# Global queries of two head pairs on 128 partitions, and two passes over the weights moved to ScalarE

## The chip, the cores and the metric

One NeuronCore of a Trainium2 chip runs the whole program. The metric is the device time of one execution in microseconds; the engines are TensorE (PE), VectorE (DVE), ScalarE (ACT), GpSimd (POOL) and SyncE (SP), which issues all DMAs here.

## What is computed

The reference takes 8 batches of 8 heads with 512 local and 32 global tokens of 64 values each, and a feed-forward part on the result.

```python
s_g = scale * q_g @ k_all.T ; out_g = sm(s_g) @ v_all
s_l = concat(scale * q_l @ k_g.T, where(abs(i - j) <= 32, scale * q_l @ k_l.T, -1e9))
out_l = sm(s_l) @ concat(v_g, v_l)
x = concat(out_g, out_l) as (8, 544, 512)
u = x + real(fft over tokens and over the 512 columns of x)
un = (u - mean(u)) / sqrt(var(u) + 1e-6)
out = u + max(un @ w_ch1, 0) @ w_ch2
```

The weights w_ch1 (512 x 2048) and w_ch2 (2048 x 512) arrive as 64-bit floats; the program reads each as two 32-bit words.

## The kernel before

The kernel works with sums of two float16 parts (a high and a low one), so a product of two matrices is three matmuls. A list of tasks is made in `run`, each with an engine, an assumed duration, the tasks it needs and the buffers it takes. `Plan.order` then writes out one fixed order for each engine's queue from these and from tables of numbers (STEP, STAG, LEAD, DLEAD, BIAS, CAPS). On the chip every queue runs in that order and waits on semaphores.

Weights: 32 tiles of 128 x 512. `w_load` brings one in as pairs of 32-bit words. `w_abs` (line 356, ScalarE) writes the absolute value of the high words to PSUM. `w_bits` takes their maximum into a column (line 363, VectorE, with an accumulator) and shifts the bits left by 3 (line 364). `w_join` puts in sign and top exponent bit (line 370) and the top 3 bits of the low word (line 371). `w_max`, `w_fold`, `w_top`, `w_spread` and `w_scale` make one scale from the maxima of four tiles (w_ch1) or of all sixteen (w_ch2); `w_hi` and `w_lo` write the two float16 parts (lines 430, 432, 439).

Attention goes by pairs of heads p (32 pairs, 4 to a batch). Local queries: `scores`, `masked` (line 607, VectorE), `exps`, `p_hi`, `p_lo`, a DMA transpose `turn`, `values` (lines 642 and 644), `norm`. Values are prepared by `v_mul`, `v_hi` (line 539, ScalarE) and `v_lo` into one of two buffers vN; keys by `prep_hi` and `prep_lo` into one of two buffers kT from the third batch on. Global queries of a pair take 64 partitions (2 heads of 32): `g_scores` (lines 668 and 669 for the first two batches, 673 and 674 after), `g_max` (679 to 681, VectorE), `g_exp` (686 and 687, ScalarE), `g_hi` (690, ScalarE), `g_lo` (693, GpSimd), the DMA transpose `g_turn`, `g_values` (708) and `g_norm` (716 to 718, VectorE).

After a batch's four pairs the transforms follow (`d_odd` to `d_addv`), with the GpSimd sums ahead and `d_lo` (line 855) and `d_tail_lo` (line 882) on VectorE. Then come the layer norm (`l_stats` to `l_turn`) and the FFN: 17 chunks of 256 rows, each in 8 steps of `f_first` (line 1038), `f_hi`, `f_lo` and `f_second` (line 1056). `f_first` uses the same two PSUM buffers (`ps1`) as the weights. The attention of later batches is woven in between the FFN steps on every queue.

Of the kernel before, what the change touches and what calls it, by code (L numbers as in the profile page):

```python
# [19 lines left out]
P = 128  # L20
# [1323 lines left out]
```

## Time and profile before

| what | us |
|---|---|
| median of 3 runs (lowest, highest) | 1085.59 (1083.68, 1087.31) |
| the profiled execution's own time | 1085.01 |
| its span, first to last instruction | 1083.2 |

The rows below come from the profiled execution. Its times run from the start of its span; a time that is measured and one of the span differ by 1.8 us.

### The profile page before, as it was taken

What the parts mean: (1) busy time and instruction counts of PE and PEld (TensorE: products, weight loads), DVE (VectorE), ACT (ScalarE), POOL (GpSimd) and SP (SyncE); (2) the same over time, 40 slices, a digit from 0 to 9 for tenths busy, and PEclk for the clock granted to TensorE, in tenths of its full rate; (3) what the DMA queues carried; (4) which work ended last, traced back from release to release, by engine and by line L of the source; (5) the groups of instructions that cost most, each with busy time, mean ns of one, the idle gap of its engine ahead of it and who ended that gap; (6) DMA issues with size and microseconds to landing.
All of it is one profiled execution on the core that took longest, in us unless ns stands there. A gap on an engine that the chain in (4) does not pass through costs nothing.

```text
span 1083.2 us, 24999 instructions
## 1 busy us (share of the span) xinstructions
PE 978.0 (90%) x9683; PEld 688.2 (64%) x9683; DVE 615.5 (57%) x1766; ACT 584.8 (54%) x1250; POOL 610.9 (56%) x840
## 2 busy tenths in 40 slices
PE   3756277998999999999999979998999999999996
PEld 2535155775767766776777747675776766676664
DVE  5999998426864585477548666647435242231111
ACT  5867467985886867786778648645212111111110
POOL 5559958886968876967877785766036020010000
PEclk9865555999999999999999989998999999999999
DMA  8999867726766858594785947384412112111000
GB/s 297 257 254 252 248 162 178 156 74 142 131 154 139 201 108 187 130 208 111 160 191 96 204 93 151 62 170 81 108 50 59 21 42 59 20 40 40 1 21 20
DMA packets 249568, 137.60 MB, mean 127 GB/s; under 512 B 200577, under 2 KB 223201, under 8 KB 249449
## 3 DMA queue, kind: packets, MB, share of 16 engines
q1 hardware_dynamic: 249448, 136.01, 55.4%
q8 instruction: 76, 1.25, 0.5%
q14 instruction: 44, 0.35, 0.1%
HBM read 65.10 MB, written 18.35 MB: 77 GB/s over the span
## 4 chain that ended last, share of the span: by engine, by line
PE 77%; DVE 14%; POOL 4%; issue 2%; DMA 2%; SPq 1%; ACT 1%; POOLq 0%; DVEq 0%; ACTq 0%
PE ps L1038 31%; PE acc L1056 30%; PE S L597 3%; PE bk L642 2%; DVE pe L607 2%; PE bk L644 2%; PE psd L930 2%; DVE ht L882 1%; DVE ps L364 1%; PE S L673 1%; DVE ps L363 1%; PE pvg L708 1%; PE S L594 1%; DVE wm L371 1%; DVE ps L370 1%
## 5 line engine op out<-in xcount | busy, mean ns | idle before, releaser
L1038 PE MATMUL ps<-uh,wh 128*128 128x256 f16 x3264 | 386.0, 275 | 0.0
L1056 PE MATMUL acc<-wh,h 128*128 128x512 f16 x1632 | 377.8, 381 | 0.0
L1038 PEld LDWEIGHTS <-wh 128*128 128x128 f16 x3264 | 316.0, 99 | 52.5 <-issue 1.2
L1056 PEld LDWEIGHTS <-h 128*128 128x128 f16 x1632 | 153.9, 98 | 166.5 <-issue 3.3
L1043 ACT ACTIVATE h<-ps 128x512 f16<-128x512 f32 x136 | 80.9, 595 | 273.2 <-PE ps L1038 272.7
L1047 DVE SCALAR_TENSOR_TENSOR h<-ps,h 128x512 f16<-128x512 f32 x136 | 93.6, 688 | 219.7 <-ACT h L1043 219.6
L624 POOL TENSOR_TENSOR ph<-pe,ph 128x448 f16<-128x448 f32 x128 | 132.1, 1046 | 88.8 <-ACT ph L620 71.2
L616 ACT ACTIVATE pe<-pe,nm 128x224 f32<-128x224 f32 x256 | 101.6, 469 | 21.5 <-DVE nm L607 21.5
L607 DVE CUSTOM_DVE_ANT_0 pe<-S,msk,z 128x224 f32<-128x224 f32 x192 | 75.3, 446 | 38.5 <-PE S L597 25.8
L642 PE MATMUL bk<-vN,pl 128*128 128x65 f16 x768 | 70.5, 203 | 20.0 <-DVE x L655 11.0
L620 ACT ACTIVATE ph<-pe 128x448 f16<-128x448 f32 x128 | 68.9, 563 | 5.9 <-DMA pl<-ph 5.3
L642 PEld LDWEIGHTS <-pl 128*128 128x128 f16 x768 | 61.8, 105 | 15.1 <-DMA pl<-ph 9.4
L644 PEld LDWEIGHTS <-pl 96*128 96x128 f16 x768 | 59.4, 104 | 14.7 <-issue 11.1
L954 POOL TENSOR_TENSOR u<-u,asm 128x257 f32<-128x257 f32 x16 | 13.1, 821 | 95.8 <-DMA u<-xs 50.1
L644 PE MATMUL bk<-vB,pl 96*128 96x65 f16 x576 | 54.4, 204 | 0.0
L693 POOL TENSOR_TENSOR pgr<-pg,pgr 64x576 f16<-64x576 f32 x32 | 41.4, 1294 | 20.7 <-issue 13.0
L543 POOL TENSOR_TENSOR vN<-vf,vN 128x640 f16<-128x640 f32 x32 | 43.5, 1361 | 14.0 <-ACT vN L539 13.7
L1061 DVE SCALAR_TENSOR_TENSOR u<-acc,ve,u 128x512 f32<-128x512 f32 x34 | 25.4, 750 | 32.3 <-PE acc L1056 32.3
L597 PEld LDWEIGHTS <-qT 64*128 64x128 f16 x1152 | 35.0, 95 | 11.7 <-issue 6.8
L439 POOL TENSOR_TENSOR wh<-wm,wh 128x512 f16<-128x512 f32 x32 | 36.9, 1158 | 4.8 <-ACT wm L432 3.5
L653 DVE TENSOR_SCALAR dn<-bk,z 128x4 f32<-128x4 f32 x64 | 13.8, 215 | 43.7 <-PE bk L644 43.7
L597 PE MATMUL S<-kT,qT 64*128 64x192 f16 x576 | 36.7, 248 | 1.8 <-DVE nm L607 1.8
(203 smaller groups left out, 1621.2 us busy)
## 6 DMA issues: line engine op xcount, KB each, us to landing
qk<-in_qk SPq DMA_DIRECT2D x32, 512.0 KB
vf<-in_v SPq DMA_DIRECT2D x32, 320.0 KB
raw<-in_moe_w_ch SPq DMA_DIRECT2D x17, 512.0 KB
xs<-x SPq DMA_DIRECT2D x32, 256.0 KB
out<-u SPq DMA_DIRECT2D x16, 512.0 KB
x<-xs SPq DMA_DIRECT2D x24, 256.0 KB
u<-xs SPq DMA_DIRECT2D x24, 256.0 KB
rw<-in_moe_w_ch SPq DMA_DIRECT2D x8, 512.0 KB
```

The source lines that it names most:

```text
L543: self.nc.gpsimd.tensor_sub(vN[:, :, 1, :, 0:64], self.st[p]["vf"], vN[:, :, 0, :, 0:64])
L597: nc.tensor.matmul(ps, qT[r, a, j], kg[r, c] if o else kT[r, k0:k0 + 192], start=m == 0, stop=m == 2)
L607: nc.vector.tensor_tensor_reduce(self.per[(4 * p + j) % 4][:, h, 0:224], S[:, h, 224 * n:224 * n + 224], self.msk[:, j], z[:, 8:9], 3e38, ...
L616: nc.scalar.activation(pe[:, h, 0:224], pe[:, h, 0:224], AF.Exp, bias=nm[:, n, h:h + 1], scale=-1.0)
L620: self.nc.scalar.activation(ph[:, 0, :, 0:224], self.per[i % 4][:, :, 0:224], AF.Copy)
L624: self.nc.gpsimd.tensor_sub(ph[:, 1, :, 0:224], self.per[i % 4][:, :, 0:224], ph[:, 0, :, 0:224])
L642: nc.tensor.matmul(pv[:, j % 2, h], pl[:, 4 * a + 2 * h], vN[:, j, c, h, :], start=m == 0, stop=False)
L644: nc.tensor.matmul(pv[:, j % 2, h], pl[0:96, 4 * a + 2 * h + 1], vb, start=False, stop=m == 2)
L1038: nc.tensor.matmul(ps[:, q], wt[:, w, c0:c0 + P], uh[:, :, 4 * a + kt, :], start=n == 0, stop=n == 11)
L1043: self.nc.scalar.activation(h[:, 0], self.fps[c, fp], AF.Relu)
L1047: self.nc.vector.scalar_tensor_tensor(h[:, 1], self.fps.pop((c, fp)), 0.0, h[:, 0], op0=ALU.max, op1=ALU.subtract)
L1056: nc.tensor.matmul(self.acc_f[c, j], h[:, a, q, j * P:(j + 1) * P], self.w[1, f][:, w, :], start=f == 0 and a == 0 and w == 0, stop=f == 1 ...
```

## The change

Three things change. First, w_abs scales the absolute value by a power of two, which puts the exponent where the shift needs it, and a new pass on ScalarE, `w_low`, makes the top 3 bits of the low word from its top byte and writes them over the low word. w_bits is a plain maximum, and w_join shifts while it joins. Second, the global queries of two pairs (a group g of four heads) share 128 partitions from g_scores to g_norm; g_out has four DMAs of 32 rows instead of two, and plg one buffer instead of two. The scale of each half is copied into one column (`zg`). Third, the tables and assumed durations that set the order are others.

```diff
-STEP = 5.93
+STEP = 6.09
-STAG = (35, 18, 18)
-LEAD = (86, 30, 32)
+STAG = (35, -6, 15)
+LEAD = (86, 32, 32)
-DLEAD = (74, 6, 32)
+DLEAD = (50, 14, 32)
...
-        self.nc.scalar.activation(m.bitcast(F32), self.raw[k, i][:, :, 1].bitcast(F32), AF.Abs)
+        self.nc.scalar.activation(m.bitcast(F32), self.raw[k, i][:, :, 1].bitcast(F32), AF.Abs, scale=2.0 ** -112)
+
+    def w_low(self, k, i):
+        raw = self.raw[k, i]
+        byte = raw.rearrange("p n t -> p (n t)").bitcast(U8).rearrange("p (n b) -> p n b", b=8)[:, :, 3]
+        self.nc.scalar.activation(raw[:, :, 0], byte, AF.Copy, bias=-15.5 / 32, scale=1.0 / 32)
 
     def w_bits(self, k, i):
...
-        g = m.bitcast(F32)
-        nc.vector.tensor_scalar(g, g, 2.0 ** -15, None, op0=ALU.max, op1=ALU.max, accum_out=self.mx[k][:, j:j + 1])
-        nc.vector.tensor_scalar(m, m, 3, 0x3FFFFFF8, op0=ALU.logical_shift_left, op1=ALU.bitwise_and)
+        nc.vector.tensor_reduce(self.mx[k][:, j:j + 1], m.bitcast(F32), axis=EX, op=ALU.max)
 
     def w_join(self, k, i):
...
-        hw, lw = raw[:, :, 1], raw[:, :, 0]
-        nc.vector.scalar_tensor_tensor(m, hw, -0x40000000, m, op0=ALU.bitwise_and, op1=ALU.bitwise_or)
-        nc.vector.scalar_tensor_tensor(w, lw, 29, m, op0=ALU.logical_shift_right, op1=ALU.bitwise_or)
+        nc.vector.scalar_tensor_tensor(m, m, 3, raw[:, :, 0], op0=ALU.logical_shift_left, op1=ALU.bitwise_or)
+        nc.vector.scalar_tensor_tensor(w, raw[:, :, 1], -0x80000000, m, op0=ALU.bitwise_and, op1=ALU.bitwise_or)
...
+            zg = self.p3.tile([P, 3], F32, name="zg", bufs=3)
+            for i in range(2):
+                flip(zg[64 * i:64 * i + 64, 0:1], t[64 * i:64 * i + 64, i])
+            self.zs[g] = zg[:, 0:1]
...
+    def g_scores(self, g, alt):
...
         for m, (a, c) in enumerate(((0, 0), (0, 1), (1, 0))):
-            nc.tensor.matmul(sg, qg[:, a], kT[:, 32 + 512 * c:544 + 512 * c], start=m == 0, stop=m == 2)
-            nc.tensor.matmul(s2, qg[:, a], s["kg"][:, c], start=m == 0, stop=m == 2)
+            for r, s in zip(rows, prs):
+                nc.tensor.matmul(sg[r], self.g[s["b"]]["T"][:, a, s["hp"], 0:64], s["kT"][:, 32 + 512 * c:544 + 512 * c], start=m == 0, stop=m == 2)
+            for r, s in zip(rows, prs):
+                nc.tensor.matmul(s2[r], self.g[s["b"]]["T"][:, a, s["hp"], 0:64], s["kg"][:, c], start=m == 0, stop=m == 2)
...
-                for h in range(2):
-                    r = slice(h * SG, h * SG + SG)
-                    nc.tensor.matmul(pv[r], pl[:n, 5 * a + c, r], vN[:n, c, w, h], start=c == 0 and m == 0, stop=c == 4 and m == 2)
+                for i in range(2):
+                    vN = self.st[2 * g + i]["v"][0]
+                    for h in range(2):
+                        r = slice(64 * i + SG * h, 64 * i + SG * h + SG)
+                        nc.tensor.matmul(pv[r], pl[:n, 5 * a + c, r], vN[:n, c, w, h], start=c == 0 and m == 0, stop=c == 4 and m == 2)
```

VectorE, at its first weight tiles, before (ps1 is PSUM, mx0 the maxima, rw and raw the loaded words, wm the joined words; L607 is the mask step):

```order
L363 TENSOR_SCALAR ps1_189,mx0_92<-ps1_189 128x512
L364 TENSOR_SCALAR ps1_189<-ps1_189 128x512
L370 SCALAR_TENSOR_TENSOR ps1_189<-rw_156,ps1_189 128x512
L371 SCALAR_TENSOR_TENSOR wm_188<-rw_156,ps1_189 128x512
L363 TENSOR_SCALAR ps1_199,mx0_92<-ps1_199 128x512
L364 TENSOR_SCALAR ps1_199<-ps1_199 128x512
L363 TENSOR_SCALAR ps1_208,mx0_92<-ps1_208 128x512
L364 TENSOR_SCALAR ps1_208<-ps1_208 128x512
L370 SCALAR_TENSOR_TENSOR ps1_199<-rw_156,ps1_199 128x512
L371 SCALAR_TENSOR_TENSOR wm_198<-rw_156,ps1_199 128x512
L607 ISA pe0_86,nm_228<-S_213,msk_63,zc_99 128x224
```

and now (L368 is w_bits, L373 and L374 are w_join, L620 the mask step):

```order
L368 TENSOR_REDUCE mx0_92<-ps1_194 128x1
L373 SCALAR_TENSOR_TENSOR ps1_194<-ps1_194,rw_156 128x512
L374 SCALAR_TENSOR_TENSOR wm_193<-rw_156,ps1_194 128x512
L368 TENSOR_REDUCE mx0_92<-ps1_202 128x1
L373 SCALAR_TENSOR_TENSOR ps1_202<-ps1_202,rw_156 128x512
L374 SCALAR_TENSOR_TENSOR wm_201<-rw_156,ps1_202 128x512
L368 TENSOR_REDUCE mx0_92<-ps1_212 128x1
L373 SCALAR_TENSOR_TENSOR ps1_212<-ps1_212,raw_159 128x512
L374 SCALAR_TENSOR_TENSOR wm_211<-raw_159,ps1_212 128x512
L620 ISA pe0_86,nm_240<-S_223,msk_63,zc_99 128x224
```

Of four instructions a tile three are left, and the reduction no longer writes ps1.

ScalarE, at the same tiles, before (L356 is w_abs, L539 is v_hi, L452 sums over the global queries and keys):

```order
L356 ACTIVATE ps1_189<-rw_156 128x512
L539 ACTIVATE vN_70<-vf1_74 128x5x2x64
L356 ACTIVATE ps1_199<-rw_156 128x512
L356 ACTIVATE ps1_208<-raw_159 128x512
L356 ACTIVATE ps1_234<-raw_161 128x512
L452 ACTIVATE junk_77,accg_80<-gn_179 128x256
```

and now (L357 is w_abs, L362 is w_low):

```order
L357 ACTIVATE ps1_194<-rw_156 128x512
L362 ACTIVATE rw_156<-rw_156 128x512
L357 ACTIVATE ps1_202<-rw_156 128x512
L362 ACTIVATE rw_156<-rw_156 128x512
L362 ACTIVATE raw_159<-raw_159 128x512
L357 ACTIVATE ps1_212<-raw_159 128x512
L362 ACTIVATE raw_161<-raw_161 128x512
L357 ACTIVATE ps1_220<-raw_161 128x512
```

Each tile has a second pass, which reads and writes the loaded words in place.

TensorE, at the first FFN matmul, before (L597 is scores, L1038 is f_first):

```order
L597 LDWEIGHTS qT_1947
L597 MATMUL S_2120<-kg0_68,qT_1947 128x32
L597 LDWEIGHTS qT_1947
L597 MATMUL S_2120<-kg0_68,qT_1947 128x32
L1038 LDWEIGHTS wh_981
L1038 MATMUL ps1_2153<-uh_2071,wh_981 128x256
```

and now (L610 is scores, L407 is the last w_spread, L1058 is f_first):

```order
L610 LDWEIGHTS qT_1945
L610 MATMUL S_2040<-kg0_68,qT_1945 128x32
L610 LDWEIGHTS qT_1945
L610 MATMUL S_2040<-kg0_68,qT_1945 128x32
L407 MATMUL vm_2009<-mxr_2031,part_64 128x1
L1058 LDWEIGHTS wh_448
L1058 MATMUL ps1_2085<-uh_1984,wh_448 128x256
```

The spread of the maximum of w_ch2 has moved ahead of the first FFN matmul; before, it stood 157 rows behind it.

## Rows read from the trace of the kernel before

**Rows 1.** Busy time by stretch: stretch, length; PE, PEld, DVE, ACT, POOL; PEclk, DMA share, GB/s.

```profile
0.00:30.00 30.00, 12.52 (x60) 9.02 (x60) 16.63 (x45) 16.06 (x34) 15.76 (x32) 1.00 0.87 297
30.00:120.00 90.00, 51.64 (x591) 40.64 (x591) 84.92 (x269) 63.61 (x136) 64.27 (x68) 0.62 1.07 253
120.00:180.30 60.30, 33.22 (x326) 27.46 (x326) 56.25 (x160) 39.70 (x87) 46.51 (x52) 0.50 0.70 170
180.30:1083.20 902.90, 880.58 (x8712) 611.05 (x8706) 457.66 (x1295) 465.44 (x996) 484.40 (x691) 0.99 0.49 106
```

**Rows 2.** Chain of waits by line, 30 to 180.3 us, then 180.3 to 1083.2 us.

```profile
by line: DVE pe L607 10.9%; DVE ps L364 9.3%; DVE ps L363 9.0%; DVE wm L371 7.8%; PE S L594 7.8%; DVE ps L370 7.5%; issue 6.8%; DVE x L655 3.1%; PE S L668 2.6%; DVE ng L679 2.4%; POOL wh L439 2.3%; POOL wm L531 1.8%; DVE bst L983 1.8%; PE p
...
by line: PE ps L1038 37.0%; PE acc L1056 36.2%; PE S L597 3.4%; PE bk L642 2.1%; PE bk L644 2.0%; PE psd L930 1.8%; PE S L673 1.8%; DVE ht L882 1.7%; PE psd L900 1.5%; PE pvg L708 1.3%; issue 1.2%; DVE eh L855 0.7%; PE psd L902 0.5%; DMA pl
```

**Rows 3.** Groups by line and shape, VectorE: busy us, mean ns; idle before, releaser.

```profile
L364 DVE TENSOR_SCALAR ps<-ps 128x512 int32<-128x512 int32 x32 | 22.4, 700 | 1.1
...
L363 DVE TENSOR_SCALAR_CACHE_REDUCE ps<-ps 128x512 f32<-128x512 f32 x32 | 22.0, 689 | 2.4 <-ACT ps L356 2.4
...
L679 DVE TENSOR_REDUCE ng<-S 64x1 f32<-64x512 f32 x22 | 14.9, 678 | 8.0 <-PE S L674 7.9
...
L718 DVE TENSOR_SCALAR xg<-pvg,dng 64x64 f32<-64x64 f32 x32 | 8.8, 276 | 1.3
...
L716 DVE TENSOR_SCALAR dng<-pvg,z 64x1 f32<-64x1 f32 x32 | 6.5, 204 | 11.4 <-PE pvg L708 11.2
L681 DVE TENSOR_SCALAR ng<-ng,z 64x1 f32<-64x1 f32 x24 | 6.4, 265 | 1.0
...
L363 DVE DVE_READ_ACCUMULATOR ps<-ps 128x1 f32 x32 | 4.4, 138 | 0.0
...
L680 DVE TENSOR_REDUCE ng<-S 64x1 f32<-64x32 f32 x22 | 3.8, 173 | 0.0
```

**Rows 4.** Groups by line and shape, ScalarE.

```profile
L690 ACT ACTIVATE pgr<-pg 64x576 f16<-64x576 f32 x32 | 21.6, 676 | 4.9 <-DMA plg<-pgr 4.5
...
L686 ACT ACTIVATE pg<-S,ng,z 64x512 f32<-64x512 f32 x20 | 15.4, 771 | 10.7 <-DVE ng L681 8.1 <-POOL pgr L693 2.5
...
L432 ACT ACTIVATE wm<-wm,wsc 128x512 f32<-128x512 f32 x16 | 11.5, 722 | 0.5
...
L356 ACT ACTIVATE ps<-raw 128x512 f32<-128x512 f32 x17 | 10.6, 621 | 14.8 <-DVE wm L371 14.8
...
L687 ACT ACTIVATE pg<-S,ng,z 64x32 f32<-64x32 f32 x20 | 7.3, 363 | 0.0
```

**Rows 5.** Groups by line and shape, GpSimd.

```profile
L693 POOL TENSOR_TENSOR pgr<-pg,pgr 64x576 f16<-64x576 f32 x32 | 41.4, 1294 | 20.7 <-issue 13.0 <-ACT pgr L690 5.7 <-POOL vf L531 0.9
```

**Rows 6.** Timeline of TensorE, 305 to 320 us: start, us.

```profile
305.32 0.40 PE L673 MATMUL S<-kT,gT 128*64 128x512 f16 x1
305.56 0.18 PE L674 MATMUL S<-kg,gT 128*64 128x32 f16 x1
305.59 0.38 PE L673 MATMUL S<-kT,gT 128*64 128x512 f16 x1
...
306.17 2.79 PE L1038 MATMUL ps<-uh,wh 128*128 128x256 f16 x24
...
319.17 0.65 PE L708 MATMUL pvg<-vN,plg 128*32 128x65 f16 x30
319.75 0.50 PE L1038 MATMUL ps<-uh,wh 128*128 128x256 f16 x3
```

**Rows 7.** Chain of waits in order of time, in three stretches: start, us.

```profile
244.85 6.18 DVE eh L855
...
634.67 8.49 DVE ht L882
...
734.78 6.82 DVE ht L882
```

**Rows 8.** Waits of ScalarE: us in total, times, longest us.

```profile
ACT vN L539 <- PE bk L644: 10.0, 8, 4.4
```

More of the change, by code (lines that the diff above doesn't have):

```diff
@@ L87, in raw_home @@
     return ("x0", "x1", "uh", "uh")[n % 4] if n < 16 else "uh" if n % 5 in (0, 2) or n > 27 else "u"
-PER = {**dict.fromkeys("scores masked exps norm".split(), 8), **dict.fromkeys("p_hi p_lo turn values".split(), 16),
+PER = {**dict.fromkeys("g_scores g_max g_exp g_hi g_lo g_turn g_values g_norm".split(), 2), **dict.fromkeys("scores masked exps norm".split(), 8), **dict.fromkeys("p_hi p_lo turn values".split(), 16),
        **dict.fromkeys("s_total scales0 scales l_stats l_guess l_un l_hi l_lo l_turn l_root f_first f_hi f_lo f_second f_end f_out".split(), 2)}
-WHOLE = ("w_load", "w_abs", "w_bits", "w_join", "w_max", "w_fold", "w_top", "w_spread", "w_scale", "w_hi", "w_lo", "load_consts", "l_load")
+WHOLE = ("w_load", "w_abs", "w_low", "w_bits", "w_join", "w_max", "w_fold", "w_top", "w_spread", "w_scale", "w_hi", "w_lo", "load_consts", "l_load")
 def stage_of(key):
@@ new lines, in g_scores, with g_max @@
+            for r, s in zip(rows, prs):
+                nc.tensor.matmul(s2[r], self.g[s["b"]]["T"][:, a, s["hp"], 0:64], s["kg"][:, c], start=m == 0, stop=m == 2)
+    def g_max(self, g):
+        nc, (sg, s2) = self.nc, self.G[g]
+        ng = self.p2.tile([P, 3], F32, name="ng")
+        nc.vector.tensor_reduce(ng[:, 0:1], sg, axis=EX, op=ALU.max)
+        nc.vector.tensor_reduce(ng[:, 1:2], s2, axis=EX, op=ALU.max)
+        nc.vector.tensor_scalar(ng[:, 2:3], ng[:, 0:1], ng[:, 1:2], self.zg[g][1], op0=ALU.max, op1=ALU.mult)
+        self.G[g] = sg, s2, ng[:, 2:3]
@@ L1088, in run @@
             add(("w_abs", n), ACT, .62, self.w_abs, k, i, after=[("w_load", n)] + slot, cls=3, new=[("ps1", "w", n)], use=[r])
-            add(("w_bits", n), DVE, 1.48, self.w_bits, k, i, after=[("w_abs", n)], use=[("ps1", "w", n)])
-            add(("w_join", n), DVE, 1.4, self.w_join, k, i, after=[("w_bits", n)], use=[r, ("ps1", "w", n)])
+            add(("w_low", n), ACT, .63, self.w_low, k, i, after=[("w_load", n)], use=[r])
+            add(("w_bits", n), DVE, .68, self.w_bits, k, i, after=[("w_abs", n)], use=[("ps1", "w", n)])
+            add(("w_join", n), DVE, 1.4, self.w_join, k, i, after=[("w_bits", n), ("w_low", n)], use=[r, ("ps1", "w", n)])
             last = n % 4 == 3 if k == 0 else n == 31
@@ L1107, in run @@
             add(("w_hi", n), ACT, 1.43 if k else .71, self.w_hi, k, i, after=pre)
[L1108 removed]
+            add(("w_lo", n), POOL, 1.16 if k else 1.87, self.w_lo, k, i, after=[("w_hi", n)])
         for b in range(B):
@@ L1185, in run @@
                 add(("norm", i), DVE, .89, self.norm, i, after=[("values", 2 * i), ("values", 2 * i + 1)], use=[bk, sc] + ([x] if half else []), new=[] if half else [x], **kw)
-            G = ("A", "g", p)
-            gs, gu = ([("load", p), ("b_load", b)], [qk, gT]) if rb else ([("lo_k", p), ("halo", p), ("b_lo", b)], [kT, kg, gT])
-            add(("g_scores", p), PE, 1.0 if rb else .7, self.g_scores, p, after=gs, seq=prev("g_scores"), use=gu, new=[G], alts=[["A"], ["acc0", "acc1"]], **kw)
@@ L1189, in run @@
-            add(("g_max", p), DVE, 1.08, self.g_max, p, after=[("g_scores", p)], use=[G] if rb else [G, sc], **kw)
-            add(("g_exp", p), ACT, 1.03, self.g_exp, p, after=[("g_max", p)], seq=prev("g_exp"), use=[G] if rb else [G, sc], new=[("pg", p)], **kw)
-            add(("g_hi", p), ACT, .67, self.g_hi, p, after=[("g_exp", p)], seq=prev("g_hi"), use=[("pg", p)], new=[("pgr", p)], **kw)
-            add(("g_lo", p), POOL, 1.3, self.g_lo, p, after=[("g_hi", p)], use=[("pg", p), ("pgr", p)], **kw)
```

145 lines of the change are left out of this document (78 added, 67 removed).

## Prediction

> **What bounds the kernel now.** I read the busy time by stage first, because the average over the whole span mixes two kernels in one. Up to 180.3 us, where the first matmul of the feed-forward part (FFN) starts, VectorE is the full engine: 84.92 of 90 us and 56.25 of 60.3 us, that is 141.2 of 150.3 us or 94% from 30 us on, while TensorE is busy 84.9 of the same 150.3 us and at a granted clock of 0.62 and 0.50 [rows 1]. After 180.3 us it is the reverse: TensorE 880.6 of 902.9 us (97.5%), VectorE 457.7 (51%), ScalarE 465.4, GpSimd 484.4 [rows 1]. The chain of waits says the same. Before 180.3 us its largest entries are VectorE's mask step and the four passes over each weight tile (lines 363, 364, 370 and 371); after it the two FFN lines alone are 73% [rows 2]. So a microsecond taken from VectorE ahead of the first FFN matmul moves that start, as far as no other engine takes over; a microsecond taken from ScalarE, VectorE or GpSimd after it buys nothing by itself, and one taken from TensorE after it counts in full.
>
> **Who could take over.** From 30 to 180.3 us ScalarE is busy 103.3 us and GpSimd 110.8 us [rows 1]. The DMA engines show a busy share of 1.07 from 30 to 120 us at 253 GB/s, 22.8 MB; from 120 to 180.3 us it is 0.70 at 170 GB/s, 10.3 MB [rows 1]. The change therefore goes from an engine at 94% towards three resources at 70 to 100%.
>
> **The weights.** Per tile VectorE ran line 363 (0.689 us, plus 0.138 us for reading out its accumulator) and line 364 (0.700 us) [rows 3]. It now runs one reduction of 512 PSUM elements, for which the same operation in g_max is the row: 0.678 us [rows 3]. Saved: 0.849 us a tile, 27.2 us for 32 tiles; all 32 reductions stand ahead of the first FFN matmul in the new order. The two passes of w_join keep their shape and each still reads one operand from PSUM, so I cost their edit at nothing. ScalarE pays one more pass a tile, w_low. No row shows a byte input or an integer output. The nearest below is line 356, which reads the same tile with the same stride: 0.621 us. The nearest above is line 432, 512 floats written to SBUF: 0.722 us [rows 4]. I take 0.62, since w_low and line 356 differ in type and destination only: 19.8 us for 32 tiles, up to 23.1. The scale put into w_abs is an argument of an instruction that runs anyway, so nothing. The shorter w_max saves one operation on one to four columns, five times; I leave it at nothing.
>
> **The global queries, before the first FFN matmul.** Half as many instructions, each on 128 partitions instead of 64 and as long in the free direction. I take the duration of a VectorE, ScalarE or GpSimd instruction as unchanged by partitions; it would have to double to lose the gain. Ahead of the first FFN matmul the order before has 9 g_max and 8 g_norm, the new one 4 and 4. VectorE: 5 x (0.678 + 0.173 + 0.265) = 5.6 us and 4 x (0.204 + 0.276), the reciprocal not counted, = 1.9 us [rows 3]. The new copies of a scale add 2 small instructions for each of 4 groups, 8 x 0.204 = 1.6 us. Net for VectorE with the weights: 27.2 + 5.6 + 1.9 - 1.6 = 33.1 us. ScalarE: 9 pairs of exponentials become 4 and 8 g_hi become 4, 5 x (0.771 + 0.363) + 4 x 0.676 = 8.4 us less [rows 4]. GpSimd: 5 x 1.294 = 6.5 us less [rows 5], a few small scale instructions more; it has 40 us to spare and stays out.
>
> **Where the first FFN matmul comes to stand.** About four tiles are handled in the first 30 us, in which VectorE has 13 us idle, so of the 33.1 us 3.4 count for nothing there. After 30 us VectorE keeps 141.2 - 29.7 = 111.5 us; ScalarE gets 103.3 + 28 x 0.62 - 8.4 = 112.3 us. At the 94% that VectorE reached, both end at 30 + 119 = 149 us. The DMA engines have 33.1 MB to move in that stretch; at the 253 GB/s of the crowded stretch that takes 131 us and ends at 161 us, at the 297 GB/s of the first 30 us it ends at 141 us. Two engines at 94% side by side, each feeding the other, and DMA near its limit will not all reach their best, so I take the middle of 149 and 161: 155 us, 25.3 us earlier. The new order also puts the last fold and spread of the weights' maximum ahead of the first FFN matmul on TensorE. That makes it wait for all 32 reductions, which the sum already counts.
>
> **After the first FFN matmul.** TensorE is the bound, so its own work counts. g_scores for one pair takes 306.17 - 305.32 = 0.85 us, six matmuls of 512 and 32 columns one behind the other (0.27 us from one 512 to the next) [rows 6]. They all use 64 columns of the array, the same ones. The new code alternates between the lower and the upper 64. g_values shows what alternating gives: 30 matmuls on two groups of 32 columns take 0.58 us, 0.019 us each, where 65 streamed columns at the 0.27 us for 544 of g_scores would take 0.032 us [rows 6]; so two groups overlap to a factor of about 1.7. I take g_scores of two pairs as 0.85 us instead of 1.70. 11 of the 12 groups with this code come after the first FFN matmul: 9.4 us less. The bound on the other side is no overlap, 0. The Trainium skill, TensorEngine Tiling (Array Packing), section Available Configurations, lists 128 x 64 as two tiles, and its Key Properties say that different tiles can load and multiply in parallel; by that rule the saving would be the same 9.4 us, and no run here shows it yet at 64 columns. g_values now alternates over four groups; it lies between 0.58 and 1.16 us for two pairs, and I take no gain (bound: 12 x 0.58 = 7 us). g_max, g_exp, g_hi, g_lo and g_norm halve on engines that are 51 to 54% busy here; the FFN matmuls hide them before and after, so nothing. Were that cover gone, the other 16 - 4 groups would be worth some 1.8 us each on ScalarE.
>
> **Sum against the profiled execution.** 1083.2 - 25.3 - 9.4 = 1048.5 us span; its own time is 1085.01, 1.8 more than its span, and the median of the runs 1085.59. Forecast 1050 us.
>
> **Rivals.**
> *DMA or the mix of engines binds, and the first stage shortens little.* For it: the share of 1.07 [rows 1]. If ScalarE and VectorE reach only 80%, the FFN starts at 30 + 112.3 / 0.8 = 170 us: 1065 us.
> *The first stage is packed better than it was.* At 100% of ScalarE's 112.3 us it starts at 142 us: 1037 us. For it: VectorE did hold 94%. Against it: DMA would have to hold 296 GB/s.
> *The two column halves do not overlap.* The order and the first stage stay: 1050 + 9.4 = 1059 us.
> *The long stalls change.* Three times after 180 us TensorE waits for one VectorE instruction that takes 6.18, 8.49 and 6.82 us [rows 7]; the three sum to 21.5 us. Others of the same lines cost nothing on the chain. GpSimd is at work without a break in each. The new order rearranges these neighbours: none left gives 1050 - 21.5 = 1029 us, twice as many 1071 us. I have no row for which, and forecast three again. The Trainium skill, GPSIMD Engine Reference, section Key points, says that GpSimd shares its SBUF interfaces with VectorE and contends with VectorE instructions that have two SBUF inputs, and these three have two; by that rule such stalls stay as likely as before, since the instructions are unchanged.
> *Slower: the pair of pairs holds its buffers.* The values (two buffers) and, later, the keys (two buffers) of both pairs are now held until g_values and g_scores of the group have run. ScalarE's v_hi of the next pair waits at the head of its queue, and behind it stand the exponentials and f_hi, for which TensorE's FFN waits. Before, v_hi waited 10.0 us for the values' matmuls in 8 waits, the longest 4.4 us [rows 8]. To end above 1088 us it must cost TensorE over 38 us, 2.4 us for each of 16 groups. Against it: ScalarE has half its time free after the start. w_low as the culprit would need 1.6 us an instruction, 2.6 times line 356.
> *The change does nothing it says* has no place here: the instructions are gone from the order.
>
> **How the numbers follow.** Forecast (1042 to 1058) 0.58; first stage shortens little 0.13; packed better 0.10; no overlap of halves 0.08; stalls change 0.07; buffers, slower 0.04. I let the range run from 1036 to 1067: it takes in all but the outer stall cases and the buffers, and some of the first rival beyond 170 us. Within 0.3%, which is about what a measurement of this kernel can tell from no change, only a piece of the first and last rivals can lie: 0.02. Faster 0.94, slower 0.04.
>
> **What would show it.** In the new profile the first FFN matmul should start at 145 to 165 us, w_low last 0.62 to 0.72 us, the reduction 0.68, and VectorE and ScalarE both be 85 to 94% busy between 30 us and that start. g_scores of a group should take 0.85 to 1.0 us. From the first FFN matmul to the end should be 893 us instead of 903. If the start is later than 170 us with ScalarE below 80%, DMA or the buffers took over; if the second stretch is not shorter, the halves do not overlap or the stalls grew.

## The result, and the profile after

| | before | after |
|---|---|---|
| median of 4 runs (lowest to highest), us | 1086.1 (1083.7 to 1087.3) | 1039.4 (1037.7 to 1040.4) |
| span of the profiled execution, us | 1083.2 | 1038.2 |
| first FFN matmul, us | 180.3 | 169.7 |
| from there to the end, us | 902.9 | 868.5 |

The ratio is 0.9571 [0.9549, 0.9594]: 46.7 us less. The time lies inside the range that was given, 10.6 us below its number. But the two parts of the sum came out the other way round: the first stage gave 10.6 us instead of 25.3, and the stretch behind it gave 34.4 instead of 9.4.

Busy time by stretch of the kernel after, in the columns of [rows 1]:

```profile
0.00:30.00 30.00, 11.35 (x65) 9.00 (x65) 16.38 (x52) 18.77 (x40) 16.09 (x32) 1.00 0.96 307
30.00:169.70 139.70, 75.65 (x899) 62.74 (x899) 113.78 (x324) 113.47 (x244) 108.09 (x119) 0.57 0.96 246
169.70:1038.20 868.50, 855.27 (x8722) 597.46 (x8721) 424.11 (x1235) 440.79 (x953) 468.08 (x698) 1.00 0.50 108
```

In the middle row VectorE and ScalarE are both busy 81% of the time (113.8 and 113.5 of 139.7 us), where VectorE alone had 94% [rows 1]. Neither is full over the whole stretch any more. In the last row TensorE is busy 98.5%, at a granted clock of 1.00.

The share of 81% is an average over pieces with different limits. Three pieces of the middle row:

```profile
50.00:70.00 20.00, 11.80 (x184) 9.92 (x185) 17.51 (x58) 19.00 (x44) 19.50 (x21) 0.67 1.08 253
70.00:90.00 20.00, 10.76 (x77) 7.83 (x75) 13.02 (x39) 12.92 (x28) 13.85 (x16) 0.57 0.87 237
150.00:169.70 19.70, 9.25 (x143) 6.63 (x139) 19.09 (x44) 15.35 (x36) 16.42 (x17) 0.50 0.75 181
```

From 50 to 70 us ScalarE is at 95% and GpSimd at 98%. From 70 to 90 us no compute engine is over 70%. In the last 19.7 us VectorE is at 97%, with the layer norm, mask steps and the maximum of w_ch2 among others. One of TensorE's two longest waits of the stretch ends there, 3.6 us before the first FFN matmul, and it is for that maximum (us in total, times, longest):

```profile
PE vm L398 <- DVE mx L392: 9.2, 1, 9.2
```

The chain of waits by line, from 30 us to the first FFN matmul and behind it:

```profile
by line: DVE pe L620 9.8%; PE S L607 9.7%; DMA raw<-in_moe_w_ch 9.4%; DVE ps L373 6.5%; issue 6.2%; DVE mx L368 5.4%; DVE wm L374 5.3%; DMA pl<-ph 4.6%; DMA u<-xs 3.8%; ACT pe L629 2.4%; ACT wh L432 2.3%; DVE unh L1026 2.1%; ACT ps L357 1.7
...
by line: PE acc L1076 35.2%; PE ps L1058 35.0%; PE S L610 3.0%; PE psd L950 2.0%; PE bk L655 2.0%; PE bk L657 1.9%; DMA pl<-ph 1.8%; issue 1.3%; PE psd L920 1.2%; DMA x<-xs 1.1%; PE S L689 0.8%; DVE eh L875 0.7%; DVE un L1017 0.6%; PE pvg L
```

Against [rows 2], the four weight passes of VectorE have shrunk from 33.6% to three with 17.2%, and transfers, which did not stand among the large entries, now hold 17.8% in three entries (weights, turns, residual). No entry reaches 10%: the stage passes from engine to engine. Behind the start, `DVE ht` (1.7% in [rows 2]) is gone from the large entries.

The groups that answer to [rows 3] to [rows 5] (VectorE, ScalarE, GpSimd):

```profile
L368 DVE TENSOR_REDUCE mx<-ps 128x1 f32<-128x512 f32 x32 | 21.8, 683 | 6.3 <-ACT ps L357 6.3
L373 DVE SCALAR_TENSOR_TENSOR ps<-ps,raw 128x512 int32<-128x512 int32 x17 | 11.7, 688 | 0.0
L696 DVE TENSOR_REDUCE ng<-S 128x1 f32<-128x512 f32 x10 | 6.9, 688 | 8.4 <-PE S L691 8.4
...
L362 ACT ACTIVATE raw<-raw 128x512 int32<-128x512 uint8 x17 | 11.2, 656 | 0.0
L703 ACT ACTIVATE pg<-S,ng,zg 128x512 f32<-128x512 f32 x10 | 7.7, 765 | 0.4 <-DVE ng L698 0.2
L707 ACT ACTIVATE pgr<-pg 128x576 f16<-128x576 f32 x16 | 10.9, 681 | 0.4
...
L710 POOL TENSOR_TENSOR pgr<-pg,pgr 128x576 f16<-128x576 f32 x16 | 20.5, 1279 | 6.4 <-ACT pgr L707 4.1 <-DMA pl<-ph 2.2
```

On 128 partitions each instruction of the global queries lasts as long as it did on 64, within 2% (0.688 against 0.678, 0.765 against 0.771, 0.681 against 0.676, 1.279 against 1.294 us). The reduction takes 0.683 us (0.678 was used), and w_low 0.656 us (0.62 was used, 0.72 the bound).

TensorE's timeline of the kernel after (start, us), one g_scores group and its next matmul, then one g_values group and its next:

```profile
246.59 0.41 PE L689 MATMUL S<-kT,gT 128*64 128x512 f16 x2
246.83 0.18 PE L691 MATMUL S<-kg,gT 128*64 128x32 f16 x2
246.86 0.39 PE L689 MATMUL S<-kT,gT 128*64 128x512 f16 x2
247.08 0.18 PE L691 MATMUL S<-kg,gT 128*64 128x32 f16 x2
247.11 0.38 PE L689 MATMUL S<-kT,gT 128*64 128x512 f16 x2
247.33 0.18 PE L691 MATMUL S<-kg,gT 128*64 128x32 f16 x2
247.44 0.20 PE L655 MATMUL bk<-vN,pl 128*128 128x65 f16 x1
...
266.06 0.66 PE L726 MATMUL pvg<-vN,plg 128*32 128x65 f16 x60
266.65 0.20 PE L655 MATMUL bk<-vN,pl 128*128 128x65 f16 x1
```

From 246.59 to 247.44 are 0.85 us for two pairs; one pair alone took as long [rows 6]. And 60 matmuls of g_values take 0.59 us, where 30 took 0.58.

**Where the 34.4 us behind the start come from.** I added up the two timelines from each start on TensorE to the next, by line, idle time apart. g_scores went from 20.0 to 9.3 us (-10.7), g_values from 13.8 to 7.2 (-6.6), idle time from 12.8 to 3.7 (-9.1), the two FFN lines from 732.9 to 726.3 (-6.6). That is 33.0 of the 34.4. Groups on TensorE behind the start (busy, mean ns, idle before and what ended it), first before, then after:

```profile
L1038 PE MATMUL ps<-uh,wh 128*128 128x256 f16 x3264 | 386.0, 275 | 0.0
L1056 PE MATMUL acc<-wh,h 128*128 128x512 f16 x1632 | 377.8, 381 | 0.0
L902 PE MATMUL psd<-c1tr,ht 96*128 96x137 f16 (+1 forms) x70 | 16.0, 229 | 9.2 <-DVE ht L882 9.2
```

```profile
L1058 PE MATMUL ps<-uh,wh 128*128 128x256 f16 x3264 | 380.6, 273 | 0.1
L1076 PE MATMUL acc<-wh,h 128*128 128x512 f16 x1632 | 375.1, 379 | 0.8 <-DVE h L1067 0.8
L922 PE MATMUL psd<-c1tr,ht 96*128 96x137 f16 (+1 forms) x70 | 15.7, 225 | 1.5 <-DVE ht L902 1.5
```

The idle time that the transform's matmuls (line 902, now 922) spent on `ht` went from 9.2 to 1.5 us. The FFN matmuls are the same 3264 and 1632, yet a little shorter on average, because the stretches of a lower clock are gone: in peek_before below, which has the order of the kernel before but no such stretches, the two lines take 727.4 us. Three stretches of 30 us of the kernel before, around the long VectorE instructions of [rows 7]:

```profile
240.00:270.00 30.00, 26.40 (x275) 18.64 (x274) 17.12 (x31) 17.72 (x38) 21.07 (x22) 0.94 0.67 138
630.00:660.00 30.00, 24.11 (x243) 17.07 (x241) 21.25 (x38) 15.14 (x32) 19.17 (x21) 0.89 0.65 136
720.00:750.00 30.00, 26.71 (x258) 18.78 (x256) 21.65 (x42) 12.70 (x24) 21.41 (x29) 0.89 0.54 120
```

TensorE was idle there for 3.3 to 5.9 us, and the granted clock over the stretch is 0.94, 0.89 and 0.89: for a part of it the lower of the two levels, 1.2 GHz. In the kernel after the same three stretches of time, in which other work stands, show 30.00 us busy at 1.00.

### The profile page after: what moved, and what is told of

Its sections match the earlier page's. It is cut to its first block, busy times and chain, and to the rows that moved or that the text cites. A ratio compares the mean times of both kernels' runs of the same rounds, so it can differ in the third digit from the quotient of the medians.

```text
span 1038.2 us, 24797 instructions
## 1 busy us (share of the span) xinstructions
PE 942.3 (91%) x9683; PEld 669.2 (64%) x9683; DVE 554.3 (53%) x1609; ACT 573.0 (55%) x1234; POOL 592.3 (57%) x848
## 4 chain that ended last, share of the span: by engine, by line
PE 71%; DVE 10%; DMA 6%; POOL 5%; ACT 3%; issue 2%; SPq 1%; POOLq 0%; DVEq 0%; ACTq 0%
PE acc L1076 29%; PE ps L1058 29%; PE S L610 3%; DMA pl<-ph 2%; DVE pe L620 2%; PE bk L655 2%; PE psd L950 2%; PE bk L657 2%; PE S L607 2%; DMA raw<-in_moe_w_ch 1%; DVE ps L373 1%; PE psd L920 1%; DMA x<-xs 1%; DMA u<-xs 1%; DVE mx L368 1%
## 5 line engine op out<-in xcount | busy, mean ns | idle before, releaser
L1058 PE MATMUL ps<-uh,wh 128*128 128x256 f16 x3264 | 380.6, 273 | 0.1
L1058 PEld LDWEIGHTS <-wh 128*128 128x128 f16 x3264 | 315.2, 98 | 51.6 <-issue 0.4
L620 DVE CUSTOM_DVE_ANT_0 pe<-S,msk,z 128x224 f32<-128x224 f32 x192 | 75.0, 446 | 25.3 <-PE S L610 20.4
L607 PE MATMUL S<-qk 64*128 64x192 f32 x128 | 30.3, 562 | 22.4 <-DVE nm L620 19.8
L610 PEld LDWEIGHTS <-qT 64*128 64x128 f16 x1152 | 34.6, 94 | 9.8 <-issue 6.3
L1022 ACT ACTIVATE unh<-un 128x512 f16<-128x512 f32 x34 | 21.2, 624 | 28.0 <-DVE un L1017 27.8
L610 PE MATMUL S<-kT,qT 64*128 64x192 f16 x576 | 36.2, 246 | 0.0
```

Of the source, the lines that this page charges most:

```text
L607: nc.tensor.matmul(ps, q[r, P * j:P * j + P], kg[r] if o else kw[r, k0:k0 + 192], start=True, stop=True)
L610: nc.tensor.matmul(ps, qT[r, a, j], kg[r, c] if o else kT[r, k0:k0 + 192], start=m == 0, stop=m == 2)
L620: nc.vector.tensor_tensor_reduce(self.per[(4 * p + j) % 4][:, h, 0:224], S[:, h, 224 * n:224 * n + 224], self.msk[:, j], z[:, 8:9], 3e38, ...
L1058: nc.tensor.matmul(ps[:, q], wt[:, w, c0:c0 + P], uh[:, :, 4 * a + kt, :], start=n == 0, stop=n == 11)
```

## The experiments

My theory after the result (A): the first stage is held by engines and queues that wait for each other, no longer by one engine; and behind the start the order took away stalls that come from GpSimd working without a break beside VectorE. Its rivals: DMA bandwidth, ScalarE or VectorE alone holds the first stage; and the new instructions, not the order, took the stalls away.

"First" is the first FFN matmul and "rest" the time from there to the end of the span, both in the profiled execution. In rows from 30 us to the first FFN matmul, the columns are those of [rows 1]. Each ratio is to runs of the kernel before made beside that version; the medians of these are the range in the first line.

| kernel | median us (ratio to before) | first | rest |
|---|---|---|---|
| before | 1084.2 to 1086.1 | 180.3 | 902.9 |
| after | 1039.4 (0.957 [0.955, 0.959]) | 169.7 | 868.5 |
| w_only: weights changed, tables of before | 1088.2 (1.002 [1.000, 1.004]) | 193.7 | 893.7 |
| g_only: pairing changed, tables of before | 1071.5 (0.987 [0.983, 0.991]) | 192.2 | 873.7 |
| old_tables: whole change, tables of before | 1068.8 (0.984 [0.981, 0.988]) | 187.8 | 880.3 |
| g_apart: after, halves one behind the other | 1044.5 (0.962 [0.959, 0.966]) | 168.0 | 871.1 |
| half_after: after, half the weight bytes | 1036.5 (0.957 [0.954, 0.961]) | 165.5 | 868.3 |
| half_before: before, half the weight bytes | 1081.6 (0.998 [0.996, 1.001]) | 179.6 | 901.3 |
| extra_after: after, every second tile loaded twice | 1098.1 (1.014 [1.010, 1.017]) | 223.2 | 874.7 |
| peek_before: before, GpSimd held at eh and ht | 1067.3 (0.986 [0.982, 0.989]) | 182.7 | 883.3 |
| low_short: after, 16 columns of low bits | 1040.6 (0.960 [0.957, 0.962]) | 167.4 | 870.7 |
| max_short: after, 16 columns in the maximum | 1036.4 (0.956 [0.953, 0.959]) | 166.8 | 870.6 |
| both_short: both | 1036.9 (0.956 [0.953, 0.959]) | 165.5 | 870.1 |
| peek_after: after, GpSimd held at eh and ht | 1038.6 (0.958 [0.955, 0.961]) | 169.7 | 867.0 |

### The parts alone: w_only, g_only, old_tables

w_only takes the new w_abs, w_low, w_bits, w_join and w_max into the kernel before; g_only takes everything on the global queries; old_tables is the whole change with the five tables of the kernel before:

```diff
-STEP = 6.09
-STAG = (35, -6, 15)
+STEP = 5.93
+STAG = (35, 18, 18)
...
-DLEAD = (50, 14, 32)
+DLEAD = (74, 6, 32)
```

> The kernel before with the change to the weights alone (scaled absolute value, low bits on ScalarE, plain maximum), tables of before; the written-out order moves a little because assumed durations differ. Theory A (the first stage is held by DMA once VectorE is relieved, so the first FFN matmul moves up by about 10 us and the rest is as before): 1076 us, within 1070 to 1081. Rival (VectorE's 27 us come off in full): 1060 us, first FFN matmul at 153 us.

> The kernel before with the global queries of two pairs together alone, tables of before. Theory A: after the first FFN matmul g_scores saves 10.7 us and g_values 6.6 us on TensorE, the first stage some 0 to 5 us: 1066 us, within 1061 to 1071, if the long stalls stay. Rival (the pairs' longer hold of buffers costs what they save): 1080 us or more.

> The whole change with the tables of before (STEP, STAG, LEAD, DLEAD and the old entries of BIAS). If the new tables are what took the stalls of 21 us away: 1055 us, with waits of over 3 us at the DFT in the chain. If the tables give nothing and the stalls go with the lighter GpSimd queue: 1040 us. If the old tables also fit the first stage badly, the first FFN matmul comes after 175 us.

Against 1085.8 us of the kernel before beside them, the parts alone gave +2.4 (no change, within its interval) and -14.3 us, and both together on the old tables -16.9. The new tables are worth another 29.4 us. Both theories missed w_only: the weights' part alone moved the start from 180.3 to 193.7 us. g_only ended just above the range of theory A. Behind the start g_scores and g_values saved the 10.7 and 6.6 us that were expected (20.0 to 9.3 and 13.8 to 7.1), but the start came 11.9 us later instead of 0 to 5 us sooner. old_tables met neither total, 1055 or 1040 us. Its start came after 175 us, as was said for tables that fit the first stage badly, and its long waits on `ht` stayed (below). The stretch from 30 us to the first FFN matmul, w_only, then old_tables:

```profile
30.00:193.70 163.70, 100.53 (x1133) 81.27 (x1131) 132.58 (x422) 138.37 (x304) 128.75 (x141) 0.55 0.98 231
```

```profile
30.00:187.80 157.80, 84.76 (x1075) 71.95 (x1072) 123.87 (x397) 130.85 (x287) 122.27 (x150) 0.56 1.00 241
```

The count of TensorE's matmuls from 30 us to the first FFN matmul is 1133 and 1075, against 899 after and 591 + 326 = 917 before [rows 1]. With new instructions and old tables the planner draws an order in which far more attention work stands ahead of the FFN: ScalarE is busy there 138.4 and 130.9 us instead of 113.5. So the tables' gain ahead of the start is work that now stands behind it, under the FFN matmuls. On the old tables ScalarE is 83 to 85% busy in the stage, about as in the kernel after.

### The overlap of the column halves: g_apart

```diff
-        for m, (a, c) in enumerate(((0, 0), (0, 1), (1, 0))):
-            for r, s in zip(rows, prs):
+        for r, s in zip(rows, prs):
+            for m, (a, c) in enumerate(((0, 0), (0, 1), (1, 0))):
...
-            for r, s in zip(rows, prs):
```

> The changed kernel with the matmuls of g_scores in another order: all of the lower 64 columns, then all of the upper 64, so that neighbours share columns; g_values stays. If neighbours on different column halves overlap and that is the saving: g_scores takes 1.5 to 1.7 us a group again instead of 0.85, 11 groups after the first FFN matmul, 1048 us. If the saving is not from overlap: 1039 us.

Neither was met: +5.1 us in the median, and a profiled span only 0.9 us longer, with a first FFN matmul 1.7 us sooner. One group on its timeline:

```profile
244.38 0.40 PE L689 MATMUL S<-kT,gT 128*64 128x512 f16 x1
244.62 0.18 PE L690 MATMUL S<-kg,gT 128*64 128x32 f16 x1
244.65 0.41 PE L689 MATMUL S<-kT,gT 128*64 128x512 f16 x2
244.87 0.21 PE L690 MATMUL S<-kg,gT 128*64 128x32 f16 x2
...
245.50 0.20 PE L655 MATMUL bk<-vN,pl 128*128 128x65 f16 x1
```

The group takes 1.12 us, not 1.70 and not 0.85: at the switch of halves the matmuls of the two still pair up (x2 at one start). Over all groups behind the start g_scores rose from 9.3 to 12.3 us. So alternating is worth 3 us against this order, and overlap also comes where it isn't written out.

### What holds the first stage: half_after, half_before, extra_after

The half kernels load only the left 256 of the 512 columns of a weight tile and use them twice (8.4 MB less, the same instructions on the same sizes); extra_after loads every second tile twice into the same buffer:

```diff
-        self.nc.sync.dma_start(raw.rearrange("p n t -> p (n t)"), self.w_src(k, i).bitcast(I32))
+        src = self.w_src(k, i).bitcast(I32)
+        self.nc.sync.dma_start(raw[:, 0:256].rearrange("p n t -> p (n t)"), src[:, 0:512])
```

```diff
         self.nc.sync.dma_start(raw.rearrange("p n t -> p (n t)"), self.w_src(k, i).bitcast(I32))
+        if n % 2:
+            self.nc.sync.dma_start(raw.rearrange("p n t -> p (n t)"), self.w_src(k, i).bitcast(I32))
```

> The changed kernel; each weight tile's DMA brings only its left 256 columns, and every pass reads these twice, so instructions and their order stay and 8.4 MB of loads are left out (the weights' right halves are not the reference's). If DMA holds the first stage: at 250 GB/s the first FFN matmul comes 20 to 33 us earlier, 137 to 150 us instead of 169.7, and the time is 1010 to 1020 us. If engines or buffers hold it: at most 5 us earlier, 1034 us or more.

> The kernel before with the same half loads (the weights' right halves are not the reference's). If VectorE holds its first stage as its 94% say: first FFN matmul at most 6 us earlier than 180.3 us, 1078 us or more. If DMA held that stage too: 20 to 33 us earlier, 1053 to 1066 us.

> The changed kernel with every second weight tile loaded twice, 8.4 MB more. If DMA holds the first stage: 20 to 33 us later, 1060 to 1072 us. If engines hold it and DMA has room: at most 5 us later, 1044 us or less.

half_after and half_before, 30 us to the first FFN matmul:

```profile
30.00:165.50 135.50, 70.09 (x900) 58.82 (x899) 112.50 (x324) 112.52 (x244) 107.83 (x119) 0.59 0.83 202
```

```profile
30.00:179.60 149.60, 83.49 (x909) 67.71 (x906) 140.66 (x425) 101.90 (x221) 110.13 (x118) 0.56 0.77 174
```

With a fifth of the stretch's bytes gone (202 GB/s over 135.5 us against 246 over 139.7) the start moves by 4.2 us after, and by 0.7 before, inside the ranges that were given for engines or buffers and for VectorE. DMA bandwidth alone is not what holds it in either kernel. In half_before VectorE is again at 94% (140.7 of 149.6), which agrees with VectorE holding the kernel before. The chain of half_after, from 30 us to its first FFN matmul, has no transfer among its large entries any more:

```profile
by line: PE S L614 13.1%; DVE pe L627 10.3%; issue 7.7%; DVE ps L380 7.6%; DVE wm L381 6.7%; DVE mx L375 6.3%; PE bk L662 3.2%; DVE unh L1033 3.0%; PE sga L691 2.8%; POOL wh L448 2.6%; PE bk L664 2.4%; DVE x L675 2.3%; POOL wm L551 2.0%; DV
```

extra_after and the waits of SP's queue in it (us in total, times, longest):

```profile
30.00:223.20 193.20, 82.76 (x919) 67.67 (x918) 119.53 (x347) 120.06 (x258) 111.90 (x124) 0.53 0.85 227
```

```profile
SPq L351 <- DMA raw<-in_moe_w_ch: 32.1, 8, 6.4
SPq L351 <- DMA rw<-in_moe_w_ch: 15.7, 3, 5.7
SPq L351 <- DMA rx<-in_moe_w_ch: 15.7, 3, 6.1
```

The start is 53.5 us later while the DMA engines are less busy than after (0.85 against 0.96). The second load waits in SP's queue until the first into its buffer has landed, 63.5 us in 14 waits, and the turns, loads and stores behind it wait with it. I had meant to add bytes, and added waits at the head of a queue instead: both expectations missed. The run says nothing on bytes. 63.5 us of waits at the head of SP's queue moved the start by 53.5, but every second weight tile was also complete later, and the run does not separate the two.

### ScalarE and VectorE in the first stage: low_short, max_short, both_short

These leave out work: w_low makes 16 columns, which are used over and over, and the reduction looks at 16 columns. 0.66 us become 0.20, and 0.68 become 0.17.

```diff
-        self.nc.scalar.activation(raw[:, :, 0], byte, AF.Copy, bias=-15.5 / 32, scale=1.0 / 32)
+        self.nc.scalar.activation(raw[:, 0:16, 0], byte[:, 0:16], AF.Copy, bias=-15.5 / 32, scale=1.0 / 32)
...
-        nc.vector.tensor_reduce(self.mx[k][:, j:j + 1], m.bitcast(F32), axis=EX, op=ALU.max)
+        nc.vector.tensor_reduce(self.mx[k][:, j:j + 1], m[:, 0:16].bitcast(F32), axis=EX, op=ALU.max)
```

> The changed kernel, with ScalarE making low bits of 16 columns of each weight tile instead of 512 (VectorE uses those 16 over and over, same sizes as before). 28 such instructions of 0.66 us stand between 30 us and the first FFN matmul at 169.7 us; some 0.5 us of each goes, 14 us of ScalarE's 113.5 us there. If ScalarE alone holds the first stage, the first FFN matmul comes 14 to 17 us sooner (153 to 156 us, 1023 to 1026 us in all). If VectorE holds it, nothing (168 to 170 us, 1037 to 1040 us). If the two hold it in turns through their in-order queues, as the chain that ended last reads (a few of these instructions stand in it), 2 to 6 us (164 to 168 us, 1033 to 1038 us).

> The changed kernel, with VectorE's reduction for a weight tile's largest value over 16 columns instead of 512. 27 of these, 0.683 us each, stand between 30 us and the first FFN matmul; some 0.55 us of each goes, 15 us of VectorE's 113.8 us there. If VectorE alone holds the stage: 15 to 18 us sooner (152 to 155 us, 1021 to 1025 us). If ScalarE holds it: nothing (168 to 170 us). If they hold it in turns (these reductions are 5.4% of the chain of that stretch, 7.5 us): 4 to 8 us (162 to 166 us, 1031 to 1036 us).

> Both cuts at once: 14 us less of ScalarE and 15 us less of VectorE between 30 us and the first FFN matmul. If one engine alone holds the stage, no more than the better of the two single cuts gives. If both hold it in turns, about the sum of the two, 7 to 14 us (156 to 163 us, 1025 to 1033 us). If the engines' sums hold it at a fixed busy share of 81%, whichever is fullest, the single cuts give next to nothing and this one 14 / 0.81 = 17 us (153 us, 1022 us). If neither does (latency of transfers and of TensorE's chain), under 4 us (166 us or later).

The start came 2.3, 2.9 and 4.2 us sooner. both_short from 30 us to the first FFN matmul:

```profile
30.00:165.50 135.50, 76.47 (x889) 62.66 (x886) 101.92 (x320) 100.23 (x243) 108.00 (x119) 0.54 0.96 250
```

12 us less of VectorE and 13 us less of ScalarE bought 4.2 us of start, and both fell to 74 or 75% busy. So neither engine's sum over the stretch holds the stage, nor do the two at a fixed busy share (that called for 153 us). low_short lies in its range for two engines in turns (2 to 6 us); max_short with 2.9 us is below its own (4 to 8), and both_short just above the range for neither engine (under 4). Two things stayed in place in both_short. The DMA engines are as busy as in the kernel after, 0.96 at 250 GB/s. And the last 19.5 us are still VectorE's, at 97%, because the passes that were cut hardly stand there:

```profile
146.00:165.50 19.50, 9.04 (x139) 6.43 (x137) 18.95 (x43) 14.56 (x35) 15.71 (x16) 0.50 0.72 181
```

In the times little of the sooner start arrives (1040.6, 1036.4 and 1036.9 against 1039.4 us, ratios that agree within their intervals): the rest grew by about 2 us in each, so that a sooner start is partly given back.

### The long VectorE instructions: peek_before, peek_after

Both put a GpSimd copy of one column behind each VectorE instruction on `eh` and `ht`; it reads that instruction's result, so GpSimd stops until it is done:

```diff
             t.fn(*t.args, *([t.alt] if len(t.alts) > 1 else []))
+            if t.key[0] in ("d_lo", "d_tail_lo"):
+                self.peek(*t.key)
...
+    def peek(self, n, b, odd=0):
+        d = self.D[b]
+        t = d["ht"][64:96, 0:1] if n == "d_tail_lo" else d["eh"][:, 1, 514 * odd:514 * odd + 1]
+        self.nc.gpsimd.tensor_copy(self.pk[64:96] if n == "d_tail_lo" else self.pk, t)
```

> The kernel before; after each d_lo and d_tail_lo (VectorE, lines 855 and 882) GpSimd has one more instruction that copies one column of what they wrote, so that GpSimd has to pause until they are through; order otherwise as before. If the three long instructions (6.18, 8.49, 6.82 us) wait for a pause of GpSimd: none of them lasts over 3 us, TensorE's idle of 12.8 us after the first FFN matmul falls to under 6 us, 1065 to 1078 us. If they wait for something else: they stay over 6 us, 1085 us or more.

> The changed kernel with a one-column GpSimd copy that reads the result behind each of the VectorE instructions on eh and ht that wait for a pause of GpSimd. After the first FFN matmul the changed kernel has 3.7 us of TensorE idle left, of which 1.5 us in front of a matmul that waits for such an instruction (ht). If the new order has already moved these waits off TensorE's path, 0 to 2 us are won and the time stays within 0.3%: 1037 to 1040 us; the mean of the eh and ht instructions falls from 1.71 and 1.25 us to 0.8 to 0.95 us. If they still cost the first stage (VectorE is one of its fuller engines), another 2 to 5 us: 1033 to 1037 us.

These instructions by shape in the kernel before, in peek_before and in old_tables (busy, mean ns):

```profile
L882 DVE SCALAR_TENSOR_TENSOR ht<-et,dsc,ht 32x513 f16<-32x513 f32 x8 | 20.3, 2537 | 3.7 <-ACT ht L877 3.5
L855 DVE SCALAR_TENSOR_TENSOR eh<-s,dsc,eh 128x512 f16<-128x512 f32 x8 | 13.4, 1673 | 1.0 <-ACT eh L851 1.0
```

```profile
L858 DVE SCALAR_TENSOR_TENSOR eh<-s,dsc,eh 128x512 f16<-128x512 f32 x8 | 9.9, 1237 | 1.3 <-ACT eh L854 1.3
L890 DVE SCALAR_TENSOR_TENSOR ht<-et,dsc,ht 32x513 f16<-32x513 f32 x8 | 6.6, 821 | 7.7 <-ACT ht L885 7.5
```

```profile
L902 DVE SCALAR_TENSOR_TENSOR ht<-et,dsc,ht 32x513 f16<-32x513 f32 x8 | 27.4, 3431 | 3.8 <-ACT ht L897 3.7
```

TensorE's wait for `ht` behind the start in old_tables (us in total, times, longest):

```profile
PE psd L922 <- DVE ht L902: 13.4, 4, 7.8
```

The timelines fit a wait for GpSimd. The three long instructions of [rows 7] end at 251.03, 643.15 and 741.59 us, each 0.55 us after a GpSimd instruction ended (250.48, 642.60 and 741.04 us). The same holds of all 13 instructions of these lines, these three among them, that last over 3 us in the kernels before and after, w_only, g_only and old_tables (0.55 to 0.59 us), and 2 to 10 other GpSimd instructions ended while they lasted. In peek_before the mean of `ht` falls from 2.54 to 0.82 us, TensorE's idle time behind the start from 12.8 to 0.9 us, and the rest from 902.9 to 883.3. The three stretches shown above are at 30.00 us busy and 1.00. So 24 one-column copies win 17 us in all (1084.2 to 1067.3) without any other change, as the first expectation had it. In old_tables `ht` takes longer than in the kernel before (3.43 us on average, 10.96 at the longest), and TensorE idles 13.4 us for it behind the start; `eh` is a little shorter there (1.02 against 1.26 us over its 16). So what took the stalls away in the kernel after is the new order, not the new instructions. In peek_after the order has already done it: the idle time falls from 3.7 to 2.2 us and the time stays the same, 1038.6 against 1039.4 us, as the first of the two expectations had it; the means of `eh` (128 x 514) and `ht` fall to 1.06 and 1.02 us, a little less far than expected. Neither it nor another version is measurably faster than the kernel after with all of its work. These copies do not reach one more place: `unh` (line 1026) takes 2.99 us at 160.95 us, ahead of the first FFN matmul, against 0.67 at its shortest, and it too ends 0.55 us after a GpSimd instruction.

## Why the prediction was right in its sum and wrong in its terms

**The first FFN matmul at 155 us: the term was mis-sized** (-10.6 instead of -25.3 us). The busy times in it were good: 111.5 us was worked out for VectorE and 113.8 measured, 112.3 for ScalarE and 113.5. What failed is the step from busy time to length, "At the 94% that VectorE reached, both end at 30 + 119 = 149 us". VectorE was at 94% where it alone was full, in the kernel before and in half_before. With its passes taken away no engine is full over the whole stretch, and both run at 81% of it. So the signs of a start at 145 to 165 us, of engines 85 to 94% busy and of 893 us behind the start were missed, while g_scores at 0.85 us, w_low at 0.656 and the reduction at 0.683 came as said. The first rival's arithmetic, 80% and 170 us, met the start, but its first cause, DMA, did not hold alone: half of the weights' bytes are worth 4.2 us. In the last 19.7 us VectorE is full again (97%), and TensorE's last long wait is for VectorE. For the 120 us ahead of that, shown is what does not hold them alone: bandwidth (half_after), ScalarE's or VectorE's sum (low_short, max_short, both_short). Each cut is worth 2 to 4 us of start, as in a chain that passes through all of them. Not excluded is that DMA and the engines limit these 120 us about equally, each taking over where the other is cut: the half loads and the short passes were not run together. What that chain waits for first is open. The transfers' 17.8% of it and extra_after may point to SP's one queue, where a turn that waits for GpSimd stands ahead of a weight load; that is argued, not shown. Against it: half_after has no transfer among its chain's large entries, and its start is only 4.2 us earlier. No run gave the turns a queue of their own.

**g_scores -9.4 us: right** (-10.7; 0.85 us a group as forecast). The Trainium skill, TensorEngine Tiling (Array Packing), lists 128 x 64 as two tiles (Available Configurations) and says that different tiles can run matmuls in parallel (Key Properties); the mean of 113 ns from the start of a matmul of 512 columns to the next matmul, where it was 234, agrees.

**g_values at no gain: mis-sized** (-6.6 us; the bound was -7). Four groups of 32 columns overlap as fully as two: 10.0 ns from one matmul to the next instead of 19.2. The Trainium skill's section Available Configurations lists 128 x 32 as four tiles; the trace agrees. To take 0 between 0 and the bound was too cautious when the rows for two groups already showed an overlap of 1.7.

**The stalls, "and forecast three again": failed.** The rival that had 0.07 came about, with 9.1 us of idle time and 6.6 us of lower clock, 15.7 of the 21.5 us that it was given. The 21.5 us were the length of the three instructions; TensorE idled 12.8 us behind them (3.6, 5.9 and 3.3), the first time for a `z` that stands behind the `eh` on VectorE. That forecast treated the stalls as bound to the instructions. They are bound to what GpSimd does beside them (peek_before), and that is set by the order, which the change also moved (old_tables). The Trainium skill, GPSIMD Engine Reference, Key points, says that GpSimd contends with VectorE instructions that have two SBUF inputs; peek_before agrees, with `ht` at 0.82 us instead of 2.54. The step from there to "as likely as before, since the instructions are unchanged" left out that the new order changes GpSimd's neighbours. How many stalls a new order has can't be read from the instructions alone. One of 6.18 us is left after (`eh`, at 222.32 us); `ht` stands behind it on VectorE, and TensorE idles 1.5 us for that.

**The pair of pairs' buffers:** the rival did not come. The waits of v_hi that answer to [rows 8], in the kernel after:

```profile
ACT vN L552 <- PE bk L657: 5.1, 3, 2.5
ACT vN L552 <- PE pvg L726: 3.2, 2, 2.2
```

[rows 8] has only the first of the two kinds for the kernel before; its waits for g_values were

```profile
ACT vN L539 <- PE pvg L708: 2.8, 3, 1.6
```

So it is 8.3 us in 5 waits against 12.8 in 11, and the part for g_values is 3.2 against 2.8 us. The 1.6 us that this rival gives for w_low as the culprit do not reach its time. With ScalarE's other 94.9 us (103.3 - 8.4) they fill it to 94% of the old 150.3 us, (141.3 - 94.9) / 28 = 1.66, which is the old start of 180 us and some 1075 us in all. For a start at 193 us and 1088 us it takes (153.2 - 94.9) / 28 = 2.1 us.

Together: 14.7 us too much forecast ahead of the start, 25.0 too little behind it (15.7 stalls and clock, 6.6 g_values, 1.3 g_scores, 1.4 not assigned). That the total came out so near is luck: two errors of opposite sign met.

## What to carry to other kernels

When a change takes work from the one full engine of a stage, don't carry its busy share over to the engines that become next: here it fell from 94 to 81%, and cuts of 12 and 13 us on two engines at once then bought 4. Read the shares in pieces, too: the average of 81% hid a last piece of 20 us at 97%, which those cuts did not touch. If long VectorE instructions stand on a path while GpSimd runs without a break, try a one-column GpSimd instruction that waits for them before rearranging anything: it was worth 17 us here. And measure a change of instructions together with its order: the weights' part alone gained nothing, and the order drawn from the old tables put more work ahead of the stage's end.

## What the hardware showed that I had not expected

- Four groups of 32 columns overlap fully: 60 matmuls of 65 columns in 0.59 us, as long as 30 on two groups.
- A VectorE instruction of 32 x 513 elements takes 0.82 us on average when GpSimd is held behind it, and up to 8.49 us beside a running GpSimd in the kernel before [rows 7], 10.96 us in old_tables. The one of 8.49 us ended 0.55 us after a GpSimd instruction did, and seven others ended while it lasted. TensorE, idle 5.9 us for it, shows a granted clock of 0.89 over the 30 us around it.
- ScalarE reads every eighth byte and writes every second 32-bit word at 0.656 us for 512, 5% above the float pass over the same tile.
